# Splitting float64 weights in six whole-word operations, and another order of the start, in an attention and FFN kernel

## The chip, the cores and the metric

The kernel runs on one core of a Trainium2 chip. The metric is the device time of one execution in microseconds (us). The engines are written as in the profile: PE is TensorE (PEld its weight loads), DVE is VectorE, ACT is ScalarE, POOL is GpSimd, SP is SyncE, which issues all the loads and stores here.

## The reference

Eight sequences of 576 tokens go through masked attention with eight heads of 64 channels. Heads 0 to 3 see a band of 32 keys ("local"), heads 4 to 7 see every 32nd key ("strided"). The result, 4608 tokens of 512 channels, goes through an FFN with 2048 hidden channels and an exact GELU:

```python
mask_local = (rel >= 0) & (rel < stride)
mask_strided = (rel >= 0) & (pos[None, :] % stride == pos[:, None] % stride)
...
attn = np.exp(scores)
attn = attn / (np.sum(attn, axis=-1, keepdims=True) + 1e-09)
return np.matmul(attn, v).astype(np.float32)
...
h = x @ w_in
g = 0.5 * h * (1.0 + erf(h * inv_sqrt2))
return (g @ w_out).astype(np.float32)
```

`w_in` and `w_out` are divided by a float64 square root when they are made, so they arrive as float64. The kernel has to turn them into float32 itself.

## The kernel before

**The work.** The FFN takes 12 tiles of 384 tokens, and each tile takes 16 chunks of 128 hidden channels. One tile and chunk is an FFN step; there are 192, counted f0 to f191. A step has four parts: 12 matmuls into a tile H (lines 541 to 543), the GELU and a rounded copy `gh` on ACT (lines 550 and 552), the rest `gl = H - gh` on DVE (line 554), and 9 matmuls into the outputs O (lines 580 to 582). H has two buffers. Every float32 factor is used as two float32r parts, a rounded one and the rest, which is why there are three matmuls where one would do, and why each activation and each weight needs a rounded copy and a subtraction.

**The attention.** A local job (L0 to L35, three to a tile) computes two blocks of 64 queries on PE, with softmax on DVE and ACT: maxima on DVE (line 208), exponentials on ACT (line 213), quotients on DVE (line 226) or ACT (line 229, four instructions), and the two parts of x on ACT (line 233) and DVE (line 235). The strided heads of tile 0 go through PE too (pieces a, b and A of the order below); those of all other tiles are done on DVE in units, dot product by dot product (lines 416 and 458). The unit job of tile 1 is called u1.

**The weights.** For each of the 16 chunks of hidden channels a float64 block of 128 partitions by 1024 words (`ws`) is loaded and split by six steps, the function `split_w`; then the two float32r parts of the chunk (`w`) stay in memory for the whole run. FFN step f of tile 0 cannot begin before chunk f is split. The six steps before are: (1) the 3 bits that float32 has below the high word's, into the low 16 bits of the low word, on DVE (line 144) or ACT (line 147); (2) the sign into the high 16 bits of the low word, on ACT (line 150) or DVE (line 152); (3) the high word, read as float32, times 2**-112, which sets the exponent, on ACT (line 156); (4) shift the high word left by 3 and or it with the low word, on DVE (line 158); (5) the rounded part, on ACT (line 162) or DVE (line 164); (6) the rest, on DVE (line 166). Lists of chunks (`LOW_V`, `SIGN_S`, `HIGH_S`) say which engine takes steps 1, 2 and 5. Steps 1 and 2 write 16-bit halves of a 64-bit word; steps 3 and 4 read and write every second 32-bit word.

**The order.** Each engine takes its instructions in program order and waits at the first that isn't ready. Up to step f15 (`NB = 16`) that order is written out by hand: the table `START` has one word for each next part of a piece, such as `c3` for the next step of splitting chunk 3, `f2` for the next part of FFN step 2, `L1`, `u1`, `w5` for the load of chunk 5, `q`, `v`, `S`, `B`, `E`, `e` for other loads. From f16 on a loop issues the steps (`step(n)`), ACT in program order and PE and DVE as a scheduler places them; this is called the steady part here. `QUOT_V` lists the local jobs of the start whose quotients are on DVE. The loaded chunks and the split ones share 17 buffers of 8 KiB a partition, given out in turn, so a late load waits for an early buffer.

Of the kernel before, what the change touches and what calls it, by code (L numbers as in the profile page):

```python
# [10 lines left out]
F32 = mybir.dt.float32  # L11
# [29 lines left out]
# The start, up to FFN step NB, in the order of each engine's instructions: a word is the next part  # L41
# of a piece of work. Loads: q and k (q) and v (v) of a local job, q and k (S) and v (B) of the strided
# heads of a tile, q and k (E) and v (e) of the first other strided heads, a chunk of weights (w).
# Pieces: local jobs (L), strided heads of a tile on the tensor engine (halves a and b, then A) and
# in units (u), splits of a chunk of weights (c), FFN steps (f).
NB = 16
START = """
    q0 L0 q1 S0 L0 L1 L1 L0 L0 L0 a0 L1 L0 L1 L1 a0 w0 b0 q2 a0 B0 v0 w1 a0 a0 a0 c0 a0 L0 b0 b0 L1
    a0 w2 b0 a0 L1 L0 b0 L0 b0 a0 b0 c0 w3 L0 b0 b0 c0 L0 a0 b0 L1 v3 L2 b0 c1 c0 L2 A0 c1 L2 L2 q3
    L2 L2 c1 L2 c1 c2 c0 L2 c1 c3 v2 A0 c2 L2 c0 c2 c1 v1 A0 L1 L2 w4 L2 A0 A0 L3 L1 L1 w5 c3 c2 c4  # L50
    L3 c4 c2 L3 c5 f0 c3 f0 L3 L3 L3 c2 v4 L3 f1 f0 c3 c4 c3 f1 L3 w6 f1 f0 c6 c6 E f0 c4 L3 c5 w7
    f2 L3 c3 c7 c4 f1 f1 L3 c5 c4 u1 f2 c6 c5 f2 q5 w8 f3 q4 f2 c7 f2 u1 c8 c5 w9 u1 f4 f3 f3 c5 f3
    c7 c9 c6 f4 f3 f5 c7 f4 c8 u1 f4 c6 c8 f5 e c9 f4 c6 f5 c8 w10 c9 c8 c7 f5 c10 f6 f6 c10 c7 f6
    c9 f5 w11 f7 f6 c10 c9 c11 f6 c11 w12 f7 u1 f7 c8 w13 c10 c11 c12 f8 f7 f7 L4 f8 c10 c11 c9 c10
    c11 L4 u1 c12 f8 L4 f8 c11 f9 c12 L4 f8 L4 f9 u1 c12 L4 f10 f9 c13 f9 L4 f10 f10 L4 w14 f9 L4
    c12 c13 u1 w15 f10 L4 u1 L4 c15 f10 f11 c12 f12 c13 u1 c14 f11 f11 c13 L5 f11 c14 c15 c14 c13
    c13 c14 f12 c15 f12 f12 c14 f11 L5 c14 v5 f13 f13 f13 c15 f12 f14 L5 f13 f13 c15 c15 L5 L5 u1
    f14 f14 f15 L5 f14 L5 f14 f15 L5 L5 u1 f15 u1 f15 L5 u1 L5 f15 f15
""".split()
# The chunks of weights whose first, second and fifth steps are on VectorE, ScalarE and ScalarE  # L60
LOW_V, SIGN_S, HIGH_S = (
    [0, 6, 10, 11],
    [0, 2, 3, 5, 6, 7, 8, 9, 10, 11, 12, 13, 14, 15],
    [0, 5, 6, 8, 9, 12, 14])
QUOT_V = (0, 2, 3, 4)   # local jobs of the start whose quotients are on VectorE
# [19 lines left out]
def attn_ffn_kernel(ctx: ExitStack, tc: tile.TileContext, qk, vl, qka, va, qs, ks, vs, w, out):  # L85
# [6 lines left out]
    NF = w.shape[0]              # hidden chunks  # L92
    NC = DM // P                 # channel chunks
# [4 lines left out]
    JPT = NJ // NTILE            # jobs of a tile  # L98
# [35 lines left out]
    def split_w(f):  # L134
        """float64 words -> the leading 24 bits in float32, in two float32r parts."""
# [3 lines left out]
        half = raw.bitcast(I16).rearrange("p (n e) -> p n e", e=4)  # L139
        byte = raw.bitcast(U8).rearrange("p (n e) -> p n e", e=8)[:, :, 3]  # L140
        hf = high.bitcast(F32)
        # low word: the 3 bits below the high word's, and the sign
        if f in LOW_V:
            nc.vector.tensor_scalar(half[:, :, 0].bitcast(U16), half[:, :, 1].bitcast(U16), 13, None,
                                    ALU.logical_shift_right)
        else:
            nc.scalar.activation(half[:, :, 0], byte, AF.Copy, scale=1.0 / 32, bias=-0.49)  # L147
        yield
        if f in SIGN_S:
            nc.scalar.activation(half[:, :, 1].bitcast(F16), hf, AF.Copy, scale=2.0 ** -60)  # L150
        else:
            nc.vector.tensor_scalar(half[:, :, 1].bitcast(U16), half[:, :, 3].bitcast(U16), 0x8000, None,
                                    ALU.bitwise_and)
        yield
        # exponent from a bias of 1023 to one of 127: the high word, read as float32, by 2**-112
        nc.scalar.activation(hf, hf, AF.Copy, scale=2.0 ** -112)  # L156
        yield
        nc.vector.scalar_tensor_tensor(high, high, 3, low, ALU.logical_shift_left, ALU.bitwise_or)
# [11 lines left out]
    # ------------------------------------------------------------------ x tiles  # L170
# [7 lines left out]
    # ------------------------------------------------------------------ local heads  # L178
# [25 lines left out]
    def softmax_parts(blocks, nq, scores, msk, p, nmax, ssum, rs, dve):  # L204
        """Four steps over blocks of scores: mask and maximum, exponentials, sums, quotients."""
# [31 lines left out]
    def local_job(x, banks=None, dve=0, pn=-1):  # L237
        """Local heads of two units: blocks (head pair, unit) of two heads' scores, [2 * LU, LK]."""
# [58 lines left out]
    def half_tile(t, o, bank):  # L297
        """Strided heads of tile t: attention of half o of the groups, [(head, query), (group, key)]."""
# [41 lines left out]
    def strided_tile(t, banks):  # L340
        """The same, attended values: [(head, query), token, channel], a bank for each row of PE tiles."""
# [23 lines left out]
    # ------------------------------------------------------------------ strided heads  # L365
# [15 lines left out]
    def load_strided(gr, nm):  # L381
        """q, k or v of the visits that share one buffer."""
# [186 lines left out]
    def ffn_o(*ns):
        """Chunks of hidden channels into the outputs, a block of tokens after another."""  # L570
# [62 lines left out]
    # a query's residue and no later: the difference's sign and lowest bits are zero  # L633
# [7 lines left out]
    # ------------------------------------------------------------------ start  # L641
# [10 lines left out]
    def job(name):  # L652
        """The parts of a piece of the start, one engine each."""
# [36 lines left out]
    active = []                  # [generator, job, stages done]  # L690
# [56 lines left out]
def lay_out(q, k, v, w_in, w_out):  # L747
    """The inputs in the order in which the chip reads them."""
# [61 lines left out]
```

## Time and profile before

| what | us |
|---|---|
| median of 3 runs | 947.9 |
| lowest, highest run | 947.17, 948.91 |
| span of the profiled execution | 946.0 |
| PE, DVE, ACT busy in the span | 905.5, 698.1, 523.7 |
| first matmul of f0 | 35.81 |
| first matmul of f16 (the steady part) | 137.49 |

The profile is of one more execution, of which the span from the first instruction to the last is known, 946.0 us; the timed runs are 1.2 to 2.9 us above it, the median 1.9. In the profile's rows a group has its line, engine, operation, tiles written and read, shapes and count, then its busy time and the mean duration of one, then the idle time of the engine ahead of it. "Busy" of PE counts overlapping matmuls: one with a duration of 0.34 us is followed by the next after 0.17.

### The profile page before, as it was taken

The page shows a single profiled execution, that of the slowest core. Times are in us where ns is not written, and L with a number is a line of the kernel's source. Part 1 is how long each engine was busy: PE and PEld are TensorE (multiplying, and loading weights), DVE is VectorE, ACT ScalarE, POOL GpSimd, SP SyncE. Part 2 cuts the span into 40 slices and gives each one's busy share as a digit, 9 for nine tenths or more (in the row PEclk, how much of TensorE's full clock was granted, in tenths as well). Part 3 has the DMA queues.
Part 4 walks back from the last instruction along what each step waited for, and adds up shares of the span by engine and source line. Part 5 has one row for each costly group of instructions (what it writes and reads, how often), then busy time and mean ns, then how long its engine had stood idle before and what let it go on. Part 6 is the DMA issues. An engine that isn't in the chain of part 4 may idle for free.

```text
span 946.0 us, 17929 instructions
## 1 busy us (share of the span) xinstructions
PE 905.5 (96%) x5588; PEld 792.6 (84%) x5588; DVE 698.1 (74%) x4831; ACT 523.7 (55%) x1113; POOL 8.1 (1%) x56
## 2 busy tenths in 40 slices
PE   4688889999999999999999999999999999999998
PEld 3576678888888888888888888888888888888997
DVE  5677689957999599678968987786999897561110
ACT  6999977545655535536535455445555544542222
POOL 1000000000000000000000000000000000000000
PEclk8599999999999999999999999999999999999999
DMA  9925320201121013002011112011211200100001
GB/s 332 338 80 200 126 82 24 73 23 57 48 73 56 24 48 105 25 23 82 24 58 60 49 29 88 23 49 47 69 32 40 90 24 1 59 1 1 34 1 34
DMA packets 21872, 62.24 MB, mean 66 GB/s; under 512 B 2576, under 2 KB 3856, under 8 KB 19728
## 3 DMA queue, kind: packets, MB, share of 16 engines
q1 hardware_dynamic: 21776, 61.09, 19.4%
q8 instruction: 44, 0.72, 0.3%
q14 instruction: 52, 0.43, 0.1%
HBM read 51.64 MB, written 9.44 MB: 65 GB/s over the span
## 4 chain that ended last, share of the span: by engine, by line
PE 87%; ACT 11%; DMA 1%; issue 1%; DVE 1%; SPq 0%; ACTq 0%
PE H L541 14%; PE H L543 14%; PE O L582 13%; PE O L581 13%; PE H L542 13%; PE O L580 13%; ACT ws L150 3%; ACT ws L147 3%; PE S_L L251 3%; PE X_L L266 2%; ACT ws L156 2%; PE S_L L257 1%; DMA qka<-in_qka_dram 1%; ACT w L162 1%; ACT H L550 1%
## 5 line engine op out<-in xcount | busy, mean ns | idle before, releaser
L541 PE MATMUL H<-xh,w 128*128 128x384 f32 x768 | 266.1, 347 | 0.9 <-ACT w L162 0.9
L543 PE MATMUL H<-xh,w 128*128 128x384 f32 x768 | 262.9, 342 | 1.1 <-DVE w L166 1.0
L550 ACT ACTIVATE H<-H 128x384 f32<-128x384 f32 x192 | 92.5, 482 | 303.0 <-PE H L543 279.4
L542 PE MATMUL H<-xl,w 128*128 128x384 f32 x768 | 260.0, 338 | 0.0
L458 DVE SCALAR_TENSOR_TENSOR acc<-sv,sc,acc 128x64 f32<-128x64 f32 x1158 | 244.3, 276 | 0.6
L580 PE MATMUL O<-w,gh 128*128 128x512 f32 x576 | 226.5, 393 | 12.7 <-ACT gh L552 12.7
L582 PE MATMUL O<-w,gl 128*128 128x512 f32 x576 | 228.4, 399 | 0.1
L581 PE MATMUL O<-w,gh 128*128 128x512 f32 x576 | 228.3, 396 | 0.0
L554 DVE TENSOR_TENSOR gl<-H,gh 128x384 fp32r<-128x384 f32 x192 | 106.0, 552 | 147.5 <-ACT gh L552 147.0
L416 DVE CUSTOM_DVE_ANT_0 junk<-sq,sk 128x64 f32<-128x64 f32 x1290 | 204.9, 216 | 0.1
L541 PEld LDWEIGHTS H<-xh,w 128*128 128x128 f32 x768 | 145.8, 190 | 11.0 <-ACT w L162 1.3
L542 PEld LDWEIGHTS H<-xl,w 128*128 128x128 f32 x768 | 145.8, 190 | 6.0 <-DVE xl L235 0.2
L543 PEld LDWEIGHTS H<-xh,w 128*128 128x128 f32 x768 | 145.5, 189 | 3.9 <-DVE w L166 2.2
L580 PEld LDWEIGHTS O<-w,gh 128*128 128x128 f32 x576 | 108.5, 188 | 32.7 <-ACT gh L552 15.1
L582 PEld LDWEIGHTS O<-w,gl 128*128 128x128 f32 x576 | 108.5, 188 | 25.4 <-DVE gl L554 3.1
L581 PEld LDWEIGHTS O<-w,gh 128*128 128x128 f32 x576 | 108.4, 188 | 18.3
L416 DVE DVE_READ_ACCUMULATOR2_ANT sc<- 128x1 f32 x1290 | 103.2, 80 | 0.0
L552 ACT CAST gh<-H 128x384 fp32r<-128x384 f32 x192 | 92.7, 483 | 5.9
L550 ACT ACT_TABLE_LOAD x38 | 48.8, 1283 | 0.7
L213 ACT ACTIVATE P_L<-P_L,nm_L 128x96 f32<-128x96 f32 x136 | 48.8, 360 | 0.0
L251 PEld LDWEIGHTS S_L<-qk 64*64 64x64 f32 x576 | 27.7, 142 | 22.9 <-issue 13.0
L426 ACT ACT_TABLE_LOAD x35 | 44.9, 1283 | 0.6
(86 smaller groups left out, 611.6 us busy)
## 6 DMA issues: line engine op xcount, KB each, us to landing
ws<-in_w_dram SPq DMA_DIRECT2D x16, 1024.0 KB, 10.1
qk<-in_qk_dram SPq DMA_DIRECT2D x36, 320.0 KB, 3.0
out_dram<-ob SPq DMA_DIRECT2D x34, 256.0 KB, 2.2
vl<-in_vl_dram SPq DMA_DIRECT2D x36, 192.0 KB, 2.7
sk<-in_ks_dram SPq DMA_DIRECT2D x8, 576.0 KB, 4.9
sv<-in_vs_dram SPq DMA_DIRECT2D x8, 576.0 KB, 3.7
sq<-in_qs_dram SPq DMA_DIRECT2D x4, 576.0 KB, 3.9
sq<-in_qs_dram SPq DMA_DIRECT2D x3, 448.0 KB, 3.6
```

The costliest lines, as they stand in the source:

```text
L251: nc.tensor.matmul(s[rows(j), cs], qv[rows(j), i, :], kv[rows(j), i, :], start=True, stop=True)
L416: nc.vector.tensor_tensor_reduce(junk, sq[vi, "q"][:, r0 + r, :], sq[vi, "k"][:, c, :], 1.0, 0.0, ALU.mult, ALU.add, ss[u][:, r, c:c + 1])
L458: nc.vector.scalar_tensor_tensor(acc[:, r, :], sq[vi, "v"][:, c, :], wgt, acc[:, r, :], ALU.mult, ALU.add)
L541: nc.tensor.matmul(hp, w1[f][:, 0, c, :], xh[:, c, :], start=(c == 0), stop=False)
L542: nc.tensor.matmul(hp, w1[f][:, 0, c, :], xl[:, c, :], start=False, stop=False)
L543: nc.tensor.matmul(hp, w1[f][:, 1, c, :], xh[:, c, :], start=False, stop=(c == NC - 1))
L550: nc.scalar.activation(hp, hp, AF.Gelu)
L552: nc.scalar.copy(gh, hp)
L554: nc.vector.tensor_tensor(gl, hp, gh.bitcast(F32), ALU.subtract)
L580: nc.tensor.matmul(o, gh[:, sl], w2[f][:, 0, :], start=(f == 0), stop=False)
L581: nc.tensor.matmul(o, gh[:, sl], w2[f][:, 1, :], start=False, stop=False)
L582: nc.tensor.matmul(o, gl[:, sl], w2[f][:, 0, :], start=False, stop=(f == NF - 1))
```

## The change

The six steps become others, which write whole 32-bit words only: (1) the low word shifted right by 29 on DVE (a 32-bit shift), or on ACT its top byte scaled by 1/32, written as a 32-bit integer; (2) the high word as float32 times 2**-112, now on DVE for one chunk; (3) on DVE, the high word shifted left by 3, or'ed with the low word, into the low word; (4) on DVE, the sign bit of the high word, or'ed with the low word, into the high word; (5) and (6) as before. The sign has no step of its own on ACT any more; it is in the second or. The lists say now: step 1 on DVE for chunk 2 alone, step 2 on DVE for chunk 10 alone, step 5 on ACT for all chunks but 9. `QUOT_V` loses job 4. The table `START` is another one with the same words (each chunk still has its six, each load and each other piece its own count); chunks are loaded in the order 0, 1, 2, 3, 5, 6, 4, 12, 9, 7, 14, 15, 8, 13, 11, 10. Comments are gone too, so that a line of the functions stands four lines higher than before (the GELU at 546, `gl` at 550) and those of `split_w` are 142 and 144 (step 1), 148 and 150 (step 2), 152, 154, 158 and 160, 162.

```diff
 START = """
-    q0 L0 q1 S0 L0 L1 L1 L0 L0 L0 a0 L1 L0 L1 L1 a0 w0 b0 q2 a0 B0 v0 w1 a0 a0 a0 c0 a0 L0 b0 b0 L1
...
+    q0 q1 S0 L0 w0 L1 L0 L0 L1 b0 v0 L1 B0 L0 L0 a0 L0 b0 q2 L0 b0 c0 a0 b0 w1 a0 L1 L0 a0 L1 b0 L0 a0
...
-LOW_V, SIGN_S, HIGH_S = (
-    [0, 6, 10, 11],
-    [0, 2, 3, 5, 6, 7, 8, 9, 10, 11, 12, 13, 14, 15],
-    [0, 5, 6, 8, 9, 12, 14])
-QUOT_V = (0, 2, 3, 4)   # local jobs of the start whose quotients are on VectorE
+LOW_V = [2]
+EXP_V = [10]
+HIGH_S = [0, 1, 2, 3, 4, 5, 6, 7, 8, 10, 11, 12, 13, 14, 15]
+QUOT_V = (0, 2, 3)
...
         if f in LOW_V:
-            nc.vector.tensor_scalar(half[:, :, 0].bitcast(U16), half[:, :, 1].bitcast(U16), 13, None,
-                                    ALU.logical_shift_right)
+            nc.vector.tensor_scalar(low, low, 29, None, ALU.logical_shift_right)
         else:
-            nc.scalar.activation(half[:, :, 0], byte, AF.Copy, scale=1.0 / 32, bias=-0.49)
-        yield
-        if f in SIGN_S:
-            nc.scalar.activation(half[:, :, 1].bitcast(F16), hf, AF.Copy, scale=2.0 ** -60)
+            nc.scalar.activation(low.bitcast(I32), byte, AF.Copy, scale=1.0 / 32, bias=-0.49)
+        yield
+
+        if f in EXP_V:
+            nc.vector.tensor_scalar(hf, hf, 2.0 ** -112, None, ALU.mult)
         else:
-            nc.vector.tensor_scalar(half[:, :, 1].bitcast(U16), half[:, :, 3].bitcast(U16), 0x8000, None,
-                                    ALU.bitwise_and)
-        yield
-        # exponent from a bias of 1023 to one of 127: the high word, read as float32, by 2**-112
-        nc.scalar.activation(hf, hf, AF.Copy, scale=2.0 ** -112)
-        yield
-        nc.vector.scalar_tensor_tensor(high, high, 3, low, ALU.logical_shift_left, ALU.bitwise_or)
+            nc.scalar.activation(hf, hf, AF.Copy, scale=2.0 ** -112)
+        yield
+        nc.vector.scalar_tensor_tensor(low, high, 3, low, ALU.logical_shift_left, ALU.bitwise_or)
+        yield
+        nc.vector.scalar_tensor_tensor(high, high, 0x80000000, low, ALU.bitwise_and, ALU.bitwise_or)
         yield
```

The first place is on ACT, where FFN step 0 reaches it. In a row stand the line, the operation, the tile written and the one read; the first number in a name is the chunk, the job or the step (`ws_3` is the loaded chunk 3, `w_0` the split chunk 0, `P_L3` belongs to local job 3, `H_0` to f0), the last one only tells tiles apart. Before:

```order
L150 ACTIVATE ws_3_327<-ws_3_327 128x1024
L147 ACTIVATE ws_4_482<-ws_4_482 128x1024
L213 ACTIVATE P_L3_495,ss_L3_498<-P_L3_495,nm_L3_497 128x96 x4
L147 ACTIVATE ws_5_510<-ws_5_510 128x1024
L156 ACTIVATE ws_3_327<-ws_3_327 128x1024
L550 ACT_TABLE_LOAD
L550 ACTIVATE H_0_527<-H_0_527 128x384
L552 CAST gh_0_541<-H_0_527 128x384
L156 ACTIVATE ws_4_482<-ws_4_482 128x1024
L550 ACTIVATE H_1_554<-H_1_554 128x384
```

Now:

```order
L158 CAST w_1_504<-ws_1_291 128x1024
L150 ACTIVATE ws_6_470<-ws_6_470 128x1024
L144 ACTIVATE ws_4_481<-ws_4_481 128x1024
L158 CAST w_3_528<-ws_3_358 128x1024
L150 ACTIVATE ws_4_481<-ws_4_481 128x1024
L546 ACT_TABLE_LOAD
L546 ACTIVATE H_0_511<-H_0_511 128x384
L158 CAST w_2_567<-ws_2_319 128x1024
L548 CAST gh_0_548<-H_0_511 128x384
L546 ACTIVATE H_1_551<-H_1_551 128x384
```

By the GELU of f0, ACT has done step 1 or 2 of seven chunks now, of six before; the exponentials of local job 3, which stood ahead of that GELU, come behind the copies of f0 and f1 and have a table load on each side.

The second place is on DVE, at the `gl` of FFN steps 4 to 6; between two rows `gl` stand the parts of chunks that DVE takes there. Before:

```order
L554 TENSOR_TENSOR gl_4_769<-H_4_746,gh_4_768 128x384
L166 TENSOR_TENSOR w_6_815<-ws_6_576,w_6_815 128x1024
L158 SCALAR_TENSOR_TENSOR ws_8_681<-ws_8_681 128x1024
L164 CAST w_7_843<-ws_7_614 128x1024
L554 TENSOR_TENSOR gl_5_819<-H_5_780,gh_5_818 128x384
L144 TENSOR_SCALAR ws_10_838<-ws_10_838 128x1024
L166 TENSOR_TENSOR w_7_843<-ws_7_614,w_7_843 128x1024
L158 SCALAR_TENSOR_TENSOR ws_9_728<-ws_9_728 128x1024
L554 TENSOR_TENSOR gl_6_861<-H_6_847,gh_6_860 128x384
```

Now:

```order
L550 TENSOR_TENSOR gl_5_832<-H_5_799,gh_5_831 128x384
L160 CAST w_9_840<-ws_9_526 128x1024
L152 SCALAR_TENSOR_TENSOR ws_11_726<-ws_11_726 128x1024
L162 TENSOR_TENSOR w_9_840<-ws_9_526,w_9_840 128x1024
L213 TENSOR_SCALAR ss_L4_781<-ss_L4_781 128x4
L154 SCALAR_TENSOR_TENSOR ws_11_726<-ws_11_726 128x1024
L148 TENSOR_SCALAR ws_10_812<-ws_10_812 128x1024
L216 RECIPROCAL rs_L4_782<-ss_L4_781 128x4
L152 SCALAR_TENSOR_TENSOR ws_10_812<-ws_10_812 128x1024
L550 TENSOR_TENSOR gl_6_870<-H_6_842,gh_6_869 128x384
```

Between two rows `gl` there stood at most three operations on 1024 words; now there are six between those of f5 and f6, among them the two ors of chunk 11 (lines 152 and 154).

More of the change, by code (lines that the diff above doesn't have):

```diff
@@ L47 @@
 START = """
-    q0 L0 q1 S0 L0 L1 L1 L0 L0 L0 a0 L1 L0 L1 L1 a0 w0 b0 q2 a0 B0 v0 w1 a0 a0 a0 c0 a0 L0 b0 b0 L1
[L49 to L58, printed above, removed]
@@ L59 @@
-""".split()
-LOW_V, SIGN_S, HIGH_S = (
-    [0, 6, 10, 11],
-    [0, 2, 3, 5, 6, 7, 8, 9, 10, 11, 12, 13, 14, 15],
-    [0, 5, 6, 8, 9, 12, 14])
-QUOT_V = (0, 2, 3, 4)
+    q0 q1 S0 L0 w0 L1 L0 L0 L1 b0 v0 L1 B0 L0 L0 a0 L0 b0 q2 L0 b0 c0 a0 b0 w1 a0 L1 L0 a0 L1 b0 L0 a0
+    b0 c0 a0 b0 a0 b0 a0 L0 b0 w2 L1 a0 b0 L0 c0 a0 L2 b0 c1 a0 v2 c0 L1 c1 w3 A0 L2 c0 c1 A0 L2 A0 v1
+    w5 L1 L2 c1 A0 L1 L2 c0 c3 v5 A0 c3 w6 L1 c5 L2 c3 L2 c5 w4 c2 L2 c3 c2 L2 L1 c6 c2 q3 L2 c5 v3 c1
+    w12 L2 c6 c1 f0 c4 c2 w9 c3 c5 c4 c3 L3 f0 f1 w7 c4 c2 L3 c4 f0 f1 w14 f1 c2 L3 f1 f0 c6 E f2 c7 L3
@@ new lines @@
+    c6 c7 w15 L3 L3 c4 c7 f0 f2 c4 w8 c7 L3 f2 f1 c5 f2 u1 L3 v4 c9 e L3 c5 f2 c9 q4 u1 w11 c7 c9 f3 c8
+    c7 L3 c8 w13 L3 f4 c9 f3 f3 c8 c6 L4 q5 f3 f4 c8 f4 f5 w10 c11 L4 c11 f4 f3 c6 f5 f5 L4 f5 c9 f6 c11
+    c9 c10 f4 L4 c11 f6 f7 c10 L4 f6 c10 L4 f6 f5 c8 c10 f7 c8 f7 L4 c12 f6 f7 c10 u1 L4 c10 f8 c12 u1
+    c11 L4 c12 c13 f9 c11 L4 f8 f8 L4 c13 f7 f8 c12 f9 f9 c13 c12 f10 f9 c14 c12 c14 f8 c13 f10 c14 f10
+    c13 f11 f10 c15 c14 f9 c15 c13 f11 u1 f11 c14 L5 f11 c15 f10 u1 L5 c14 f12 L5 u1 f11 L5 f12 u1 L5 u1
@@ L66 @@
+    L5 f13 f12 c15 L5 f12 f13 u1 f13 f14 L5 c15 f13 u1 L5 f14 f12 f14 L5 c15 L5 f15 f14 u1 f13 u1 f15 u1
+    f15 f14 f15 f15 f15
+""".split()
+LOW_V = [2]
+EXP_V = [10]
+HIGH_S = [0, 1, 2, 3, 4, 5, 6, 7, 8, 10, 11, 12, 13, 14, 15]
+QUOT_V = (0, 2, 3)
 ROWS = [(vi, b, r) for vi, (b, r0, r1) in enumerate(VISITS) for r in range(r0, r1)]
@@ L138, in split_w @@
         high, low = word[:, :, 1], word[:, :, 0]
-        half = raw.bitcast(I16).rearrange("p (n e) -> p n e", e=4)
         byte = raw.bitcast(U8).rearrange("p (n e) -> p n e", e=8)[:, :, 3]
```

## Prediction

> **What bounds the kernel now.** I read the page first: the shares of the chain that ended last, and the busy tenths in 40 slices of 23.65 us.
>
> ```profile
> PE 87%; ACT 11%; DMA 1%; issue 1%; DVE 1%; SPq 0%; ACTq 0%
> PE   4688889999999999999999999999999999999998
> DVE  5677689957999599678968987786999897561110
> ACT  6999977545655535536535455445555544542222
> ```
>
> The chain is PE's but for 11% on ACT, and ACT is full in the first five slices alone, where PE is not. The chain in order of time says that these are one stretch; its longest pieces begin and end so:
>
> ```profile
> 14.99 2.38 ACT ws L150
> 17.58 1.02 ACT ws L156
> 19.06 2.41 ACT ws L147
> ...
> 115.89 2.52 ACT ws L150 x2
> 120.37 1.21 ACT ws L156
> 121.58 0.38 ACT H L550
> 121.96 1.07 ACT ws L156
> 123.45 0.50 PE O L580
> ```
>
> From 15 to 123 us the chain runs through ACT's steps on weights, then through PE to the end. The busy times by stretch (the columns: PE, PEld, DVE, ACT, POOL with instructions, PE's granted clock, DMA share, GB/s) show who has room:
>
> ```profile
> 0.00:134.50 134.50, 97.80 (x787) 79.66 (x787) 90.56 (x286) 124.68 (x166) 3.87 (x25) 0.87 0.54 192
> 5.67:133.70 128.03, 94.97 (x762) 77.11 (x761) 88.64 (x277) 122.59 (x163) 0.47 (x3) 0.87 0.53 189
> 14.90:122.60 107.70, 79.87 (x564) 64.62 (x564) 71.88 (x204) 107.21 (x117) 0.00 (x0) 0.84 0.54 191
> 17.60:134.50 116.90, 89.28 (x599) 72.92 (x599) 82.03 (x248) 115.56 (x140) 0.47 (x3) 0.86 0.48 170
> 122.60:134.50 11.90, 11.05 (x55) 9.51 (x55) 11.24 (x49) 11.04 (x27) 0.47 (x3) 1.00 0.13 34
> 137.50:209.00 71.50, 71.50 (x443) 62.28 (x442) 57.93 (x505) 39.67 (x99) 0.40 (x3) 1.00 0.18 56
> ```
>
> From 14.9 to 122.6 us ACT works 107.21 of 107.70 us, DVE 71.88. From 137.5 on PE never waits. The timeline of PE gives the first matmul of f0, of f16 and of f32, and that of DVE the `gl` of f15:
>
> ```profile
> 35.81 0.69 PE L541 MATMUL H<-xh,w 128*128 128x384 f32 x1
> 133.99 0.55 DVE L554 TENSOR_TENSOR gl<-H,gh 128x384 fp32r<-128x384 f32 x1
> 137.49 0.51 PE L541 MATMUL H<-xh,w 128*128 128x384 f32 x2
> 209.02 0.33 PE L541 MATMUL H<-xh,w 128*128 128x384 f32 x1
> ```
>
> So the first 16 steps take 137.5 - 35.8 = 101.7 us, and the next 16, with as many local jobs (three), 71.5. What lies behind f16 is 946.0 - 137.5 = 808.5 us of PE at its own pace, and I keep it: the time after is the new start of f16 plus 808.5, plus the 1.9 us by which the median (947.9) is above the span.
>
> **The change part by part.** The rows of the split, by line and shape:
>
> ```profile
> L150 ACT ACTIVATE ws<-ws 128x1024 f16<-128x1024 f32 x14 | 35.3, 2564 | 0.0
> L147 ACT ACTIVATE ws<-ws 128x1024 int16<-128x1024 uint8 x12 | 30.5, 2544 | 0.0
> L156 ACT ACTIVATE ws<-ws 128x1024 f32<-128x1024 f32 x16 | 18.8, 1176 | 0.2
> L162 ACT CAST w<-ws 128x1024 fp32r<-128x1024 f32 x7 | 8.3, 1179 | 0.0
> L158 DVE SCALAR_TENSOR_TENSOR ws<-ws 128x1024 uint32<-128x1024 uint32 x16 | 19.5, 1226 | 5.3 <-ACT ws L156 5.3
> L164 DVE CAST w<-ws 128x1024 fp32r<-128x1024 f32 x9 | 6.2, 693 | 0.1
> L144 DVE TENSOR_SCALAR ws<-ws 128x1024 uint16<-128x1024 uint16 x4 | 5.3, 1335 | 0.0
> L152 DVE TENSOR_SCALAR ws<-ws 128x1024 uint16<-128x1024 uint16 x2 | 2.6, 1305 | 3.0 <-ACT ws L147 3.0
> L229 ACT ACTIVATE P_L<-P_L,rs_L 128x96 f32<-128x96 f32 x124 | 36.4, 367 | 0.3 <-DVE rs_L L220 0.3
> L226 DVE TENSOR_TENSOR P_L<-P_L,rs_L 128x384 f32<-128x384 f32 x3 | 1.7, 555 | 0.1
> L550 ACT ACT_TABLE_LOAD x38 | 48.8, 1283 | 0.7
> ```
>
> *ACT's price.* L150 and L156 read the same float32 words at the same step; only the write differs, two bytes against four, and it is 2564 against 1176 ns. L147 reads single bytes and writes two, and costs no more than L150. So on ACT it is the two-byte write that costs, and the new first step (bytes read, 32-bit integers written) has 1176 ns as its lower bound and 2544 as its upper. I take 1176, since the row with four-byte writes is the nearest in what it writes. The Trainium skill, "ScalarE: Activation LUTs", section "What ACT_TABLE_LOAD costs", has 186 ns and 0.833 ns an element for every function, float32 and bfloat16 alike, an estimate of 1.04 us at 1024 elements; by it the two-byte writes would cost no more than others and ACT would gain only the four operations fewer, some 4 us. The trace disagrees, with 2564 and 2544 ns.
>
> *ACT's sum.* Before: 14 x 2.564 + 12 x 2.544 + 16 x 1.176 + 7 x 1.179 = 93.5 us. Now: 15 + 15 operations at 1.176 and 15 at 1.179 = 53.0. The quotients of local job 4 come to ACT: 4 x 0.367 = 1.5. The order has eight table loads up to the copy of f15 instead of six: 2 x 1.283 = 2.6. Together 53.0 - 93.5 + 1.5 + 2.6 = -36.4 us. From its first exponential at 5.67 to the end of that copy at 133.7 ACT worked 122.59 and waited 5.4. With the same waits it would be done at 5.67 + 5.4 + 86.2 = 97.3 us. ACT ceases to be the bound.
>
> *DVE's sum.* Step 4 is an or more for each chunk: 16 x 1.226 = +19.6, if it costs what L158 costs, which reads and writes the same words (both sources and the output at every second word, two operators). Eight roundings leave: 8 x 0.693 = -5.5. Four first steps at 1.335 become one (bounds 0.69, as L164, and 1.335, which I take): -4.0. Two signs leave: -2.6. One multiplication comes (0.69 as L164 to 1.226 as L158; I take 1.2): +1.2. The quotients of job 4: -0.6. Sum +8.1 us. The order also puts eight more dot products of the steady part (8 x 0.216) and three splits of u1 (3 x 0.416) ahead of the `gl` of f15:
>
> ```profile
> L416 DVE CUSTOM_DVE_ANT_0 junk<-sq,sk 128x64 f32<-128x64 f32 x1290 | 204.9, 216 | 0.1
> L235 DVE TENSOR_TENSOR xl<-xs,xh 128x256 fp32r<-128x256 f32 x29 | 12.1, 416 | 0.0
> ```
>
> That is 3.0 more. A rule speaks against the ors: the Trainium skill, "Vector Engine (DVE) Microarchitecture Reference", section "Measured stream behaviour on trn2", has full rate only where consecutive words come in adjacent pairs, and 1.98 ns a column where all three streams hop at every element. By it, as an estimate, each or would be 2.1 us and the start 14 us or more longer on DVE. The trace disagrees: L158 takes every second word on all three streams, in 1226 ns, so the rule gets no chance of its own.
>
> *Which floor is highest.* PE: f0 to f16 cannot take less than the 71.5 us that the next 16 steps take with PE full, so f16 starts at 35.8 + 71.5 = 107.3 at the earliest, if f0 starts as before. It does about: the x of local job 2, which it needs, has eight ors in front of it on DVE, two before, but no ACT step of 2.5 us in front of it any more. ACT: 97.3 and the 3.8 from its copy to f16, 101.1. DVE: up to 17.6 us, where the chunks start on it, it waits for loads, PE and ACT; there the row of L0 on ACT stood behind an L150 of 2.48 us and now stands behind an operation of 1.18, so that this point moves 1.3 us forward, to 16.3. From there DVE worked 82.03 us of 116.9 up to the `gl` of f15, and now has 82.0 + 8.1 + 3.0 = 93.1. Without any wait it ends at 109.4, and f16 follows 3.0 later (134.5 to 137.5, the 9 matmuls of f15 and what stands ahead of them): 112.4. DVE becomes the bound of the start.
>
> *What DVE will wait.* It won't be full: the second or waits for the first, the subtraction for ACT's rounding, each `gl` for ACT's copy, all in one queue with the dot products of u1 behind them. The one stretch of the start where DVE had its work at hand is 122.6 to 134.5: 11.24 of 11.90, 94%. I take that: 16.3 + 93.1 / 0.94 = 115.3, plus 3.0 = 118.4 (rounded up). f16 starts 137.5 - 118.4 = 19.1 us earlier. Span 946.0 - 19.1 = 926.9; median 926.9 + 1.9 = **928.8 us**.
>
> *Edits at nothing.* The loads stand in another order, chunk 0 ahead of the values of the first jobs. The DMA engines were 54% busy and moved 192 GB/s up to 134.5 us; the same bytes in 115 us are 225 GB/s, and 379 were moved at the best:
>
> ```profile
> 5.67:14.90 9.23, 4.84 (x146) 3.49 (x144) 6.32 (x30) 5.14 (x24) 0.00 (x0) 1.00 1.02 379
> ```
>
> If that cover were gone, a chunk of 1 MB at 379 GB/s would add 2.8 us once. In the steady part DVE is busy 57.93 of 71.50 us between f16 and f32, and has less to do there by the 3.0 that came forward; PE keeps the lead.
>
> **The rivals.**
>
> *A: the byte read costs as much as the two-byte write.* Then the first step stays at 2544: 15 x 1.368 = 20.5 us more on ACT, 97.3 + 20.5 + 3.8 = 121.6 with ACT never waiting for the busier DVE, and some 3 us more with it: f16 at about 125, 12.5 earlier, 935.4 us. For it: no row reads bytes and writes words. Against it: L147 is not slower than L150, which reads words.
>
> *B: hardly any waits.* DVE is full from 16.3 on, and the 3.0 us of work that came forward finds room in DVE's waits: f16 at 109.4, near PE's 107.3, 28.1 earlier: 919.8 us. For it: ACT was full to 99.5% in its stretch before. Against: ACT could be that only because DVE and PE had room; now DVE needs 93 us, ACT 81 and PE 72 of some 100.
>
> *C: slower, DVE falls behind.* Between ACT's multiplication and ACT's rounding lie two ors of 1.226 us instead of one, with the `gl` that PE waits for queued behind them (six operations on 1024 words between two `gl`). If DVE waits for ACT and ACT for DVE in turn, DVE is busy a smaller share. It decides at 93.1 / (137.5 - 3.0 - 16.3) = 79%: below that the start is longer than before. At the share that DVE had, 82.03 / 116.9 = 70%, f16 starts at 16.3 + 133 + 3.0 = 152.3, and the time is 962.7 us. Against it: DVE's share was low since ACT, full, was late; ACT now has 36 us less.
>
> *D: no change.* The stretch in front of f16 isn't what the time is made of, and PE gives back later what it gains. Then 947.9. Against it: PE has no idle time behind 137.5, so that nothing there can take the gain up but DVE, which has 13.6 us of room in the first 16 steps of the steady part.
>
> **How the numbers follow.** The forecast has 0.66, A 0.14, B 0.14, C 0.04, D 0.02. A measurement of this kernel can tell about 0.2%, 1.9 us, from no change. The low end is 919, just under B. The high end is DVE at 85%, halfway between 94% and the 79% of C: 16.3 + 109.5 + 3.0 = 128.8, 8.7 earlier, 939.2, so 939; A lies inside. Outside are C, D and some of the edges. Faster by over 0.2%: 0.94; within: 0.02; slower: 0.04.
>
> **What would show it.** Right: the rows of ACT's three steps on `ws` and `w` at 1.1 to 1.2 us each, 45 of them, 53 us together; two rows of ors on DVE with 16 each at 1.2 us; f0 at 34 to 37 us and f16 at 113 to 124; DVE busy over 85% between 17 us and the `gl` of f15, ACT about 80%; in the chain, DVE in ACT's place up to some 115 us; behind f16, 808 us as before. Wrong: a first step on ACT at 2.5 us (A); DVE under 80% busy and PE waiting for `gl` (C); an or over 1.4 us; f16 early but more than 812 us behind it (D).

## The result and the profile after

| what | before | now |
|---|---|---|
| median of 4 runs, us | 947.6 | 928.28 |
| lowest, highest run | 947.17, 948.91 | 926.5, 928.66 |
| span of the profiled execution | 946.0 | 926.2 |
| first matmul of f0, f3, f16, f32 | 35.8, 54.4, 137.49, 209.0 | 35.85, 57.82, 116.67, 189.20 |
| from f16 to the end | 808.5 | 809.5 |

The ratio is 0.9788 (95% interval 0.9776 to 0.9799): 19.3 us faster by the medians. In the profiles f16 starts 20.8 us earlier and what lies behind it takes 1.0 longer. That 1.0 lies between f16 and f32; from f32 to the end both profiles take 737.0 us. Most of it is work that changed sides of the mark: seven of f15's nine matmuls into O now stand behind the first one of f16, and 16 short matmuls of a later local job ahead of it (434 matmuls in the record from f16 to f32, before 443). Their starts in the timelines give, as an estimate, 7 x 0.23 - 0.81 = 0.8 us.

From the page of the changed kernel, the shares of the chain that ended last and the tenths in 40 slices, now of 23.16 us:

```profile
PE 94%; DMA 3%; ACT 2%; SPq 0%; issue 0%
PE   4499999999999999999999999999999999999998
DVE  6899998578994999669959967968999897661110
ACT  6899675356555554446445435436455445542322
PEclk9699999999999999999999999999999999999999
DMA  9991122011030112002201121011202100100001
```

PE is full from the third slice on, of before from the seventh. The DMA engines are full for three slices. The chain in order of time shows the same:

```profile
3.54 11.71 DMA qk<-in_qk_dram
15.27 19.00 DMA ws<-in_w_dram
34.29 1.25 ACT ws L144
...
53.46 1.03 ACT w L158
54.49 0.49 ACT PT_L L255
55.02 0.69 PE S_L L262 x16
```

It goes through loads to 34 us, through ACT to 55, and through PE from there to the end. The timeline of PE has the starts of f0, f3, f16 and f32:

```profile
35.85 0.69 PE L537 MATMUL H<-xh,w 128*128 128x384 f32 x1 [2.60 <-ACT xh L229]
57.82 0.33 PE L537 MATMUL H<-xh,w 128*128 128x384 f32 x1
116.67 0.34 PE L537 MATMUL H<-xh,w 128*128 128x384 f32 x1
189.20 0.33 PE L537 MATMUL H<-xh,w 128*128 128x384 f32 x1
```

The busy times by stretch (columns as in the prediction): from the chunks' first operation on DVE to the `gl` of f15, from the first exponential to the copy of f15, f0 to f3, f3 to f16, f16 to f32.

```profile
16.30:113.50 97.20, 81.91 (x618) 71.26 (x616) 90.70 (x272) 84.22 (x145) 0.47 (x3) 0.88 0.64 218
5.67:112.20 106.53, 85.55 (x773) 74.56 (x770) 95.58 (x295) 91.01 (x168) 0.47 (x3) 0.89 0.68 234
35.85:57.80 21.95, 18.52 (x99) 16.07 (x100) 20.80 (x61) 21.80 (x31) 0.00 (x0) 0.84 1.01 352
57.80:116.67 58.87, 58.85 (x356) 51.69 (x354) 55.85 (x209) 47.62 (x87) 0.47 (x3) 1.00 0.33 119
116.67:189.20 72.53, 72.53 (x434) 63.23 (x433) 56.84 (x482) 40.56 (x100) 0.39 (x3) 1.00 0.17 55
```

Two rows matter most. From f3 to f16 PE is busy 58.85 of 58.87 us at full clock: there it is its own bound, and 13/16 of 72.53 is 58.9. From f0 to f3 it takes 21.95 us where 3/16 of 72.53 is 13.6; there ACT is busy 21.80, DVE 20.80, the DMA engines throughout. The 8.3 us too much can be taken apart, as an estimate from that row: PE waits 21.95 - 18.52 = 3.4; the clock of 0.84 costs 21.95 x 0.16 = 3.5 (the trace has it at 0.50 from f0 to 39.66 us and from 46.48 to 49.90, and PE works all through both); and the work at full clock, 18.52 - 3.5 = 15.0, is 1.4 more than an even share, since local job 3's part on PE lies there.

The rows of the split (by line and shape):

```profile
L144 ACT ACTIVATE ws<-ws 128x1024 int32<-128x1024 uint8 x15 | 17.8, 1184 | 9.9 <-DMA ws<-in_w_dram 9.8
L150 ACT ACTIVATE ws<-ws 128x1024 f32<-128x1024 f32 x15 | 17.4, 1158 | 0.0
L158 ACT CAST w<-ws 128x1024 fp32r<-128x1024 f32 x15 | 17.3, 1155 | 0.3 <-DVE ws L154 0.3
L152 DVE SCALAR_TENSOR_TENSOR ws<-ws 128x1024 uint32<-128x1024 uint32 x16 | 19.5, 1221 | 3.1 <-ACT ws L150 2.9
L154 DVE SCALAR_TENSOR_TENSOR ws<-ws 128x1024 uint32<-128x1024 uint32 x16 | 19.4, 1217 | 0.0
L142 DVE TENSOR_SCALAR ws<-ws 128x1024 uint32<-128x1024 uint32 x1 | 0.7, 686 | 0.0
L148 DVE TENSOR_SCALAR ws<-ws 128x1024 f32<-128x1024 f32 x1 | 0.7, 686 | 0.0
```

Every operation of ACT on a chunk now takes 1.16 to 1.18 us; the second or costs what the first does. ACT waits 9.8 us for chunks that are not loaded yet; before, its rows of the split showed 0.2 us of idle time in all. The waits of PE from 30 to 118 us, and how long they were in all, how often, and the longest:

```profile
PE S_L L262 <- ACT PT_L L255: 4.2, 2, 3.8
PE H L537 <- DVE gl L550: 3.0, 1, 3.0
PE H L537 <- ACT xh L229: 2.6, 1, 2.6
```

All but 0.4 us lie ahead of f0 or at f2: for local job 2's copied quotients (3.8) and its x, which f0 needs, and for a `gl` that frees H for f2.

### The profile page after: what moved, and what is told of

It is laid out like the page before. It is cut to its first block, busy times and chain, and to the rows that moved or that the text cites. A ratio compares the mean times of both kernels' runs of the same rounds, so it can differ in the third digit from the quotient of the medians.

```text
span 926.2 us, 17928 instructions
## 1 busy us (share of the span) xinstructions
PE 897.7 (97%) x5588; PEld 791.2 (85%) x5588; DVE 703.7 (76%) x4834; ACT 490.6 (53%) x1115; POOL 8.0 (1%) x56
## 4 chain that ended last, share of the span: by engine, by line
PE 94%; DMA 3%; ACT 2%; SPq 0%; issue 0%
PE H L537 15%; PE H L539 15%; PE O L578 14%; PE O L577 14%; PE H L538 14%; PE O L576 14%; PE S_L L247 3%; DMA ws<-in_w_dram 2%; PE X_L L262 2%; PE S_L L253 2%; DMA qk<-in_qk_dram 1%; ACT w L158 1%; ACT ws L144 0%; ACT L546 0%; ACT ws L150 0%; PE S_L L262 0%
## 5 line engine op out<-in xcount | busy, mean ns | idle before, releaser
L578 PEld LDWEIGHTS O<-w,gl 128*128 128x128 f32 x576 | 107.9, 187 | 22.7
L255 ACT COPY PT_L<-S_L 96x512 f32<-96x512 f32 x34 | 19.8, 582 | 46.3 <-PE S_L L253 46.3
```

The lines of the kernel that those rows point to most:

```text
L578: nc.tensor.matmul(o, gl[:, sl], w2[f][:, 0, :], start=False, stop=(f == NF - 1))
```

## The experiments

Three theories stood at first. *VectorE* (the prediction): its 93 us of work set f16. *Loads*: the full DMA engines hold the chunks back. *PE*: from f3 on PE is at its floor, and only f0 and what is lost up to f3 count. Each experiment is the changed kernel with one edit, unless it says otherwise; its ratio is to the kernel before on the same chip, with the 95% interval; f0, f3, f16 are from one profile each.

| kernel | median us | ratio (interval) | f0, f3, f16 |
|---|---|---|---|
| the change | 928.28 | 0.9788 (0.9776 to 0.9799) | 35.9, 57.8, 116.7 |
| the change, once more | 925.71 | 0.9769 (0.9751 to 0.9786) | 33.4, 57.6, 116.3 |
| old order, new operations | 928.08 | 0.9787 (0.9766 to 0.9809) | 33.6, 49.8, 118.4 |
| new order, old operations | 964.02 | 1.0164 (1.0143 to 1.0185) | 43.9, 72.7, 152.4 |
| one or | 924.94 | 0.9752 (0.9728 to 0.9776) | 34.2, 56.5, 114.5 |
| three ors | 940.62 | 0.9924 (0.9909 to 0.9938) | 35.3, 61.3, 132.9 |
| no first step | 925.09 | 0.9762 (0.9744 to 0.9779) | 34.1, 56.6, 115.5 |
| half the loads | 926.48 | 0.9776 (0.9757 to 0.9795) | 33.4, 57.9, 116.7 |
| half the loads, one or, no first step | 922.83 | 0.9728 (0.9706 to 0.9749) | 32.1, 54.8, 112.8 |
| x earlier | 928.71 | 0.979 (0.977 to 0.9811) | 32.1, 55.5, 114.3 |
| `gl` earlier | 927.17 | 0.9784 (0.9768 to 0.98) | 33.4, 56.9, 116.3 |
| x and `gl` earlier | 928.54 | 0.9799 (0.9783 to 0.9814) | 32.0, 56.9, 116.2 |

**The two halves of the change.** First the new operations and lists under the old table:

```diff
 START = """
-    q0 q1 S0 L0 w0 L1 L0 L0 L1 b0 v0 L1 B0 L0 L0 a0 L0 b0 q2 L0 b0 c0 a0 b0 w1 a0 L1 L0 a0 L1 b0 L0 a0
...
+    q0 L0 q1 S0 L0 L1 L1 L0 L0 L0 a0 L1 L0 L1 L1 a0 w0 b0 q2 a0 B0 v0 w1 a0 a0 a0 c0 a0 L0 b0 b0 L1
...
-QUOT_V = (0, 2, 3)
+QUOT_V = (0, 2, 3, 4)
```

> The new six operations and their engines in the old order of the start (old table, old choice for the quotients). If the operations bring the gain, ScalarE is rid of some 36 us of weight work here too and f16 starts at 115 to 125 us: 927 to 937 us. If the order brings it, the old one keeps the late places of its loads and splits, and the time stays over 940 us.

Then the kernel before with the new table and the new `QUOT_V`, its six old steps and lists kept.

> The old six operations (two-byte writes, 49 of them on ScalarE) in the new order of the start. If the operations bring the gain, ScalarE is full again with 93 us of weight work and the time is 945 to 955 us. If the order brings it, it is under 938 us.

Measured: 0.9787 (0.9766 to 0.9809) and 1.0164 (1.0143 to 1.0185). The operations with their lists bring the whole gain under the old table; the new table alone loses 1.6%, and at 964.02 us more than the 945 to 955 expected. The new operations under the old lists were not tried, so what the lists do alone is not shown. Stretches of the two, f3 to f16 under the old table, and from the first exponential on with the old operations:

```profile
49.80:118.37 68.57, 63.56 (x355) 53.17 (x354) 64.38 (x220) 53.31 (x89) 0.47 (x3) 1.00 0.36 132
```

```profile
5.67:148.00 142.33, 98.60 (x774) 83.56 (x771) 89.73 (x294) 130.03 (x172) 0.47 (x3) 0.90 0.50 175
```

The old table reaches f3 8.0 us earlier, but then takes 68.57 us to f16, in which PE works 63.56 and waits 5.0; the new one has more of PE's work ahead of f3 and no wait behind it. They come to f16 within 1.7 us of each other. With the old operations ACT stays the fullest engine: it works 130.03 us where it worked 122.59 (job 4's quotients and two more table loads are among it), and waits 12.3 where it waited 5.4.

**Is VectorE the bound?** One or: the second or is left out, and with it 19.5 us on DVE.

```diff
-        nc.vector.scalar_tensor_tensor(low, high, 3, low, ALU.logical_shift_left, ALU.bitwise_or)
+        nc.vector.scalar_tensor_tensor(high, high, 3, low, ALU.logical_shift_left, ALU.bitwise_or)
         yield
-        nc.vector.scalar_tensor_tensor(high, high, 0x80000000, low, ALU.bitwise_and, ALU.bitwise_or)
         yield
```

> The changed kernel without its second or on VectorE (16 operations of 1.22 us, 19.5 us); the sign of the weights is left out. If VectorE's work sets the start of f16 (theory of the prediction), f16 comes from 116.7 to 107 to 110 us, held then by TensorE's floor: 919 to 922 us. If the early loads set f0 and TensorE is near its floor behind that (rival), f16 moves by 2 us at most: 926 to 928 us.

Three ors: the second or stands twice, which adds as much.

```diff
-        nc.vector.scalar_tensor_tensor(high, high, 0x80000000, low, ALU.bitwise_and, ALU.bitwise_or)
+        for _ in range(2):
+            nc.vector.scalar_tensor_tensor(high, high, 0x80000000, low, ALU.bitwise_and, ALU.bitwise_or)
```

> The changed kernel with its second or done twice (19.5 us more on VectorE, same result). If VectorE's work sets f16, all of it shows: f16 19 to 21 us later, 946 to 950 us. If VectorE has only the waits of this start as room beside a bound that is elsewhere (6.5 us from 16.3 to 113.5), 13 us of it show: 939 to 943 us.

Measured: 924.94 and 940.62 us. f0 to f3 and f3 to f16 of one or, then of three ors:

```profile
34.20:56.50 22.30, 18.97 (x100) 15.85 (x101) 16.52 (x57) 21.73 (x31) 0.00 (x0) 0.81 1.03 371
56.50:114.47 57.97, 57.97 (x354) 50.97 (x352) 47.24 (x200) 47.24 (x87) 0.47 (x3) 1.00 0.34 117
```

```profile
35.30:61.30 26.00, 19.80 (x99) 16.51 (x100) 25.79 (x50) 23.60 (x33) 0.00 (x0) 0.93 1.03 367
61.30:132.86 71.56, 64.85 (x362) 55.50 (x360) 70.78 (x286) 48.44 (x88) 0.47 (x3) 0.95 0.23 78
```

With one or DVE has 10.7 us of room between f3 and f16 and the stretch is 0.9 us shorter, no more: PE fills it. f0 to f3 takes 22.30 us with DVE busy 16.52 of them. f16 came 2.2 us earlier, not at the 107 to 110 us that the theory asked for. So VectorE isn't what sets f16. With three ors it is: 70.78 of 71.56 us busy, PE waiting, f16 16.2 us later. Of these 3.0 come back behind f16 (939.4 - 132.86 = 806.5 us, with all of f15's matmuls ahead of the mark again), so the span is 13.2 longer; the time, 12.3 by the medians, is in the range expected of a bound elsewhere. DVE stands just under PE in the changed kernel; work taken from it brings nothing to speak of, work put on it costs after the first 7 us or so (19.5 - 12.3).

**Is it the loads, or ACT?** Half of each chunk is loaded, the rest is filled by POOL:

```diff
-        nc.sync.dma_start(wst[f], w[f])
+        nc.sync.dma_start(wst[f][:, 0:DM], w[f, :, 0:DM])
+        nc.gpsimd.memset(wst[f].bitcast(F32)[:, 2 * DM:], 0.0)
```

> The changed kernel with half of each chunk's load; the other half, w_out, is filled with zeros by GpSimd, so that the output is zero. If the loads hold the start (DMA engines full from 10 to 69 us, ScalarE waiting 9.8 us for chunks, f0 waiting for the x of job 2 behind them), f0 comes to 30 us or less and f16 3 to 7 us earlier: 921 to 925 us. If VectorE's work sets f16, f16 moves by 2 us at most: 926 to 928 us.

No first step: the 3 low bits are left out, and with them 17.8 us on ACT. The first or takes the high word on both sides in their place, so the weights come out wrong, at the same cost on DVE.

```diff
-        if f in LOW_V:
-            nc.vector.tensor_scalar(low, low, 29, None, ALU.logical_shift_right)
-        else:
-            nc.scalar.activation(low.bitcast(I32), byte, AF.Copy, scale=1.0 / 32, bias=-0.49)
         yield
...
-        nc.vector.scalar_tensor_tensor(low, high, 3, low, ALU.logical_shift_left, ALU.bitwise_or)
+        nc.vector.scalar_tensor_tensor(low, high, 3, high, ALU.logical_shift_left, ALU.bitwise_or)
```

> The changed kernel without the first step of the split (17.8 us less on ScalarE, 0.7 on VectorE); the 3 lowest bits of the weights are wrong. If ScalarE still holds the start somewhere (full from 40 to 60 us), f16 comes 3 us or more earlier: 925 us or less. If not, it moves by 1.5 us at most: 926.5 to 928.5 us.

And the three together: half the loads, one or, no first step (the one or left takes the high word on both sides).

> Half of each chunk's load, one or, no first step: all three engines' weight work cut at once; output zero. If TensorE's floor from f0 (72.5 us for 16 steps in the steady part) is then what is left, f0 is at 28 to 31 us, f16 at 101 to 105, and the time 911 to 916 us. If waits between the engines' queues hold the start whatever their work is, f16 stays over 108 us: over 919 us.

Measured: 926.48, 925.09 and 922.83 us. The first is not a clean test, since POOL's fills made job 0 later (its transposes on PE begin at 14.4 us instead of 11.2) and DVE busier in the start (102.8 us up to the `gl` of f15 instead of 98.0). f0 to f3 of no first step, then of the three together:

```profile
34.10:56.60 22.50, 18.80 (x100) 15.82 (x101) 22.26 (x63) 19.47 (x29) 0.00 (x0) 0.80 0.99 361
```

```profile
32.10:54.80 22.70, 18.39 (x100) 15.36 (x101) 17.31 (x58) 19.80 (x30) 1.91 (x2) 0.82 0.65 197
```

Relieving DVE leaves ACT full (21.73 of 22.30), relieving ACT leaves DVE full (22.26 of 22.50). Relieving both, and the loads, brings f16 3.9 us forward, while f0 comes 3.75 earlier (35.85 to 32.1; against the second profile below 3.6 and 1.3); f0 to f3 still takes 22.7 us. None of the three is the bound by itself, and the theory that PE's floor would then be what is left (f16 at 101 to 105 us) fails too.

**Can the start be moved?** x earlier: the values of jobs 1 and 2 loaded ahead of chunks 1 and 2, three steps on chunks 5 and 6 put behind job 2's softmax (the words `v1`, `v2` are gone at their later places).

```diff
-    b0 c0 a0 b0 w1 a0 L1
+    b0 c0 a0 b0 v1 w1 a0 L1
...
-    L0 b0 w2 L1
+    L0 b0 v2 w2 L1
...
-    w6 L1 c5 L2 c3 L2 c5 w4 c2 L2 c3
+    w6 L1 L2 c3 L2 w4 c2 L2 c5 c5 c3
...
-    L1 c6 c2 q3 L2 c5 v3 c1 w12 L2 c6 c1 f0
+    L1 c2 q3 L2 c5 v3 c1 w12 L2 c6 c6 c1 f0
```

> The changed kernel with the x of local jobs 1 and 2 freed from the loads of weights: their values are loaded ahead of chunks 1 and 2, and on ScalarE the first steps of chunks 5 and 6 come behind the copy and the x of job 2. If VectorE's work sets f16, f0 starts up to 5 us earlier but f16 moves by 2 us at most: 926 to 929 us. If the early loads set f0 and f0 sets f16, both move by 3 to 6 us: 922 to 925 us.

`gl` earlier:

```diff
-    w12 L2 c6 c1 f0 c4 c2 w9 c3 c5 c4 c3 L3 f0 f1 w7 c4 c2 L3 c4 f0 f1 w14 f1 c2 L3 f1 f0 c6 E f2 c7 L3
+    w12 L2 c6 c1 f0 c4 c2 w9 c3 c5 c2 c3 c2 L3 f0 f0 f1 w7 L3 f0 f1 f1 w14 f1 c4 L3 c4 c4 c6 E f2 c7 L3
```

> The changed kernel with ten words of the table moved around f0 and f1: the rounding and subtraction of chunk 2 stand ahead of f0's GELU, and the first and second or of chunk 4 (and its multiplication) behind f1's gl, so that the gl of f0 finds VectorE free. Theory (PE sets f16 from f3 on, and what is lost between f0 and f3, 3.0 us of waiting for that gl and about 1.9 us of half clock behind it, is lost for good): the wait of f2's first matmul falls to 1.5 us or less, f0 to f3 takes 18 to 20.5 us instead of 21.9, and f16 comes 1.5 to 4 us earlier, 924.5 to 927 us. Rival (VectorE's queue sets f16, 93 us of work whatever stands where): f16 within 1 us of 116.7, 927.5 to 929 us.

Both edits:

> The moves of early_x and of early_gl together. Theory (start of f0, and what is lost between f0 and f3, add up ahead of a PE that is full from f3 on): f0 at 32 to 34 us, f16 at 111 to 114, 922.5 to 926 us, the fastest of the kernels that do all the work. Rival (VectorE's queue sets f16): f16 not before 114 and 926 to 929 us, as early_x.

The changed kernel as it is, beside these two:

> The changed kernel, unchanged, beside the two above: 927 to 929.5 us. How far its f0 (35.85), f3 (57.8) and f16 (116.67) come out elsewhere in a second profile says how large a difference of single profiles means something: I expect f0 within 2 us and f16 within 2.

Measured: 928.71, 927.17, 928.54, and 925.71 for the unchanged one, below the 927 to 929.5 expected of it. No version beats it; for both edits together the theory had 922.5 to 926. In its profile, the fastest of five runs at 925.6 us, x earlier has f0 3.8, f3 2.3 and f16 2.4 us earlier; by its median nothing of that is left. The waits of PE from 30 to 118 us with `gl` earlier:

```profile
PE S_L L253 <- DVE P_L L222: 3.5, 1, 3.5
PE S_L L262 <- ACT PT_L L255: 2.8, 1, 2.8
PE H L537 <- ACT xh L229: 1.2, 1, 1.2
PE H L538 <- DVE xl L231: 0.7, 1, 0.7
PE H L537 <- DVE gl L550: 0.5, 1, 0.5
```

The edit did what it should: the wait for `gl` went from 3.0 us (1.7 in the second profile of the unchanged kernel) to 0.5. But a wait of 3.5 us for local job 3's quotients took its place, and f3 came 0.7 us earlier, f16 no more than 0.4. My theory that what is lost at that wait is lost for good falls. The second profile of the unchanged kernel says the same of f0:

```profile
33.39:57.62 24.23, 19.72 (x99) 16.11 (x100) 23.29 (x63) 23.49 (x34) 0.00 (x0) 0.79 1.02 374
57.62:116.34 58.72, 58.72 (x356) 51.64 (x354) 54.56 (x208) 46.28 (x85) 0.47 (x3) 1.00 0.29 99
```

Here f0 is 2.5 us earlier by itself, and f3 only 0.2. PE does the same work from f0 to f3 (99 matmuls in the record of both), so the lead goes into waits (4.5 us instead of 3.4) and a lower clock (0.79 instead of 0.84). The largest of these waits, 2.1 us, is for the copied quotients of job 3, as the 3.5 us with `gl` earlier were for its quotients: its transposes and products precede f3 on PE, and its softmax passes through ACT and DVE in turn, in queues that are full with chunks. That job 3 is the cause isn't shown by this; in the first profile 3.0 of the 3.4 us are the wait for `gl`.

**Why ACT's steps were slow.** Single instructions, nothing beside them: `src` is one chunk, and the outputs of 16 bits stand at every fourth, every second or every half word.

```diff
+        nc.scalar.activation(half(o[0], 4), hf, AF.Copy, scale=2.0 ** -60)
...
+        nc.scalar.activation(half(o[0], 2), hf, AF.Copy, scale=2.0 ** -60)
...
+        nc.scalar.activation(half(o[0], 1), hf, AF.Copy, scale=2.0 ** -60)
```

> No attention and no FFN: single instructions on 128 partitions by 1024 elements, six times each, nothing else running, one line for each kind. On ACT copies with a scale: float32 at every second word to 16-bit at every fourth half word (the old second step), to 16-bit at every second half word, to 16-bit packed, packed float32 to packed 16-bit, float32 at every second word to the same, packed to packed, bytes to 16-bit at every fourth half word (the old first step), bytes to 32-bit at every second word (the new first step). Theory (the write of two bytes in its scattered form costs, not the type): the scattered 16-bit writes 2.5 us, the packed ones and all 32-bit ones 1.1 to 1.2. Rival (16-bit outputs cost whatever their step): all 16-bit writes 2.5 us. Third (it is the surroundings, DMA and VectorE on the same memory): all eight at 1.1 to 1.2 us here. On VectorE: the 16-bit shift at every fourth half word 1.3 us, the 32-bit shift at every second word 0.69, the or 1.22, the copy 0.69.

Measured, by line (L115, L117 and L119 are these three in this order; L123 the same words to float32 at every second word, L121 packed float32 to packed 16 bits, L127 and L129 the old and the new first step, L132 and L134 the old and the new one on DVE, L136 the or):

```profile
L127 ACT ACTIVATE o<-src 128x1024 int16<-128x1024 uint8 x6 | 14.8, 2465 | 0.2
L115 ACT ACTIVATE o<-src 128x1024 f16<-128x1024 f32 x6 | 14.8, 2465 | 0.2
L117 ACT ACTIVATE o<-src 128x1024 f16<-128x1024 f32 x6 | 8.1, 1342 | 0.2
L132 DVE TENSOR_SCALAR o<-src 128x1024 uint16<-128x1024 uint16 x6 | 7.8, 1299 | 73.3 <-issue 73.2
L136 DVE SCALAR_TENSOR_TENSOR o<-src 128x1024 uint32<-128x1024 uint32 x6 | 7.4, 1226 | 0.2
...
L119 ACT ACTIVATE o<-src 128x1024 f16<-128x1024 f32 x6 | 6.6, 1107 | 0.2
L123 ACT ACTIVATE o<-src 128x1024 f32<-128x1024 f32 x6 | 6.6, 1099 | 0.2
L129 ACT ACTIVATE o<-src 128x1024 int32<-128x1024 uint8 x6 | 6.6, 1099 | 0.2
L121 ACT ACTIVATE o<-flat 128x1024 f16<-128x1024 f32 x6 | 6.3, 1056 | 0.2
...
L134 DVE TENSOR_SCALAR o<-src 128x1024 uint32<-128x1024 uint32 x6 | 4.2, 696 | 0.2
```

The first theory holds and the other two fall: 16 bits packed cost 1107 ns, at every second half word 1342, at every fourth 2465, and what is read makes next to no difference (bytes and float32 words cost the same, packed words 50 ns less). It isn't the surroundings either: in the kernel the rows of these operations are some 0.1 us longer, but there they overlap (below), and here they don't (the six of L117, 1342 ns each, take 8.21 us in the timeline).

## Why the prediction was right or wrong

The time was right (928.8 forecast, 928.28 measured, 925.71 in the second measurement), f16 was forecast at 118.4 and came at 116.67. The way to it was right in part. That the number came this close is luck: it was worked out from a bound, DVE over the whole start, that is not the one the runs show.

- **ACT's price: right.** 1184, 1158 and 1155 ns where 1176 to 1179 were taken; rival A falls. "It is the two-byte write that costs" was too wide: it is the two-byte write at every fourth half word, 2465 ns against 1107 packed.
- **ACT's sum: 4.8 us off.** Forecast -36.4, measured 122.59 to 91.01 = -31.6. The rows' durations overlap: L158 has 1155 ns in its row, and in the chain its successor begins 1.03 us after it (53.46 to 54.49); I subtracted durations from a busy time that counts overlap once. "Done at 97.3" also took the old waits; ACT made the copy of f15 at 112.2, since it now waits for chunks (9.8 us) and for others. From 16.3 to 113.5 us it is busy 84.22 / 97.20 = 87%, where about 80% was expected.
- **DVE's sum: right in size.** 93.1 us forecast, 90.70 measured; 94% busy forecast, 90.70 / 97.20 = 93%. Within it the first step and the multiplication on DVE were taken at 1.335 and 1.2 us and cost 0.686 each, their lower bounds.
- **"DVE becomes the bound of the start": this step failed.** DVE is as busy as forecast, and still f16 doesn't follow from it: 19.5 us less on DVE moved f16 by 2.2 us in single profiles, and the time by 1.6 to 3.4 (by the ratios, against the two measurements of the changed kernel). I took the highest of three floors over the whole stretch (PE 107.3, DVE 112.4) and put waits on top of the highest one. What the runs show is two stretches: f0 to f3, 21.95 us, where ACT and DVE are both full and yet neither alone sets the length, and f3 to f16, where PE is full and sets it. PE's floor of 107.3 was missed by 9.4 us: 8.3 from f0 to f3, and 1.0 because the 16 steps from f16, which give the measure, now take 72.53 us instead of 71.5. That DVE at 94% gives nearly the same f16 is because its work and PE's are within a few us of each other, which the three ors show from the other side: 12.3 of 19.5 us came through.
- **"DVE in ACT's place up to some 115 us" in the chain: wrong** for the same reason. There are loads to 34 us, ACT to 55, PE behind it.
- **f0 as before: right** (35.85), though a second profile of the same kernel has 33.39. How little it can matter I had not seen: f3 comes at 57.6 to 57.8 in both. It isn't nothing always: with x earlier f0 is at 32.1 and f3 at 55.5.
- **Loads at nothing: the cover was gone, but the price was not paid.** The DMA engines are full (share 1.01 at 352 GB/s from f0 to f3) and ACT waits 9.8 us for chunks. Yet f0 isn't later, and with half the loads f16 is where it was (a test that POOL's fills blur). The last loads of the new table are 8, 11, 13 and 10, in this order, and not as listed under the change.
- **Behind f16: 809.5 forecast as 808.5.** Rival D falls: 1.0 us came back between f16 and f32, most of it work that moved over the mark, and none behind f32.
- **Rival B** (919.8) asked for a DVE that is never late; a kernel with 19.5 us less on DVE, 17.8 less on ACT and half the loads comes to 922.83. **Rival C** needed DVE under 79% busy; it is at 93%, and with a third or at 70.78 / 71.56 = 99% from f3 to f16. The two ors in a row didn't make DVE and ACT wait for each other: DVE waited 3.1 and 1.4 us ahead of the first ors and the `gl`s in all.
- **The high end of the range:** 85% is not halfway between 94% and 79%; that is 86.5%, and 937 us instead of 939. Nothing else hangs on it.

**Open.** What holds f0 to f3 at 22 to 24 us when DVE, ACT and the DMA engines all have room (22.7 us, busy 17.31 and 19.80, share 0.65) is settled in part. PE itself is busy 18.39 of these 22.70 us, at half clock up to 40.22 us; the other 4.3 are waits for the `gl` of f0 (1.7), for x ahead of f0's second matmul (1.5) and for job 3's copied quotients (1.1). No single one of these is shown to be the cause. Other profiles have other waits there, up to 3.5 us for job 3's quotients; taking job 3 out of that place, or a third H buffer, was not tried. The unchanged kernel gave 928.28 and 925.71 in two measurements, each against the kernel before on its own chip, so the 1.8 to 3.3 us by which one or, no first step and half the loads lie below 928.28 can't be told from scatter. f16 is no better witness: in the seven profiles whose matmuls stand alike around f16 (the change twice, half the loads, no first step, x earlier, `gl` earlier and both), the run's time is f16 plus 811.3 us, so the unchanged kernel's eight runs, 924.69 to 928.66 us, stand for f16 between 113.4 and 117.3, as an estimate. The three together, whose slowest run is 923.67, lie clear of that.

## What to carry to other kernels

Find the floors stretch by stretch, not over a whole start: a kernel can go from loads to a stretch where two engines are full and neither alone sets the time, and on to a full PE, within 60 us, and a sum for one engine over all of it can hit the time for a wrong reason. That an engine is 93% busy does not make it the bound; take some of its work away and see what moves, and put some on to see how much room it has. When an operation writes scattered half words, price the same operation with whole words first.

## What the runs showed of the hardware that was not expected

- On ACT the cost of a 16-bit output goes by its step: 1107, 1342 and 2465 ns for 1024 elements packed, at every second and at every fourth half word. The Trainium skill, "ScalarE: Activation LUTs", section "What ACT_TABLE_LOAD costs", has 186 ns and 0.833 an element, 1039 ns here as an estimate: the packed rows are near it (1107, and 1056 with packed words read), the scattered 16-bit ones are not. The same section has back-to-back operations overlap by about 93 ns; the kernel's trace agrees in kind, with L158's 1155 ns followed after 1.03 us; the single instructions do not overlap.
- On DVE the shift of one 32-bit word in two took 696 ns alone and 686 in the kernel, that of one half word in four 1299: the old form was slow on both engines.
- PE waited 3.0 us for `gl` up to 46.13 us; in the 4 us behind it its granted clock was 0.57:

```profile
46.00:50.00 4.00, 3.87 (x13) 3.87 (x14) 3.60 (x7) 3.99 (x11) 0.00 (x0) 0.57 0.95 334
```

So this wait cost PE 3.87 x 0.43 = 1.7 us more behind it, as an estimate from this row. The Trainium skill, "TensorE: Matmul & The Clock Gate", section "The HAM clock gate", has the clock halved after an idle window of some 3.4 us and full again after as long a busy one; the trace agrees in the lower clock and in its length (0.50 from 46.48 to 49.90 us, 3.4 us), though the wait of 3.0 us is shorter than such a window.
